# Loading each head pair's q, k and v one batch ahead in a fused sparse-attention and MLP kernel

## The chip, the cores and the metric

The kernel runs on one core of a Trainium2 chip. The metric is the device time of one execution in microseconds (us). A core has engines that work in order, each on its own stream of instructions: TensorE (PE, with its weight loads PEld), VectorE (DVE), ScalarE (ACT), GpSimd (POOL) and SyncE (SP). They wait for one another through semaphores. Transfers between DRAM and the on-chip memory are issued here by POOL (all loads) and SP (all stores).

## The reference

Attention over 8 batches, 8 heads, 576 positions of 64 channels. Heads 0 to 3 see only the last 32 positions (local); heads 4 to 7 see only earlier positions with the same remainder modulo 32 (strided). The heads' outputs, side by side, are the 4608 tokens of an MLP with a squared ReLU.

```python
B, H, S, D = q.shape                      # 8, 8, 576, 64
scores = (1.0 / np.sqrt(D)) * np.matmul(q, k.transpose(0, 1, 3, 2))
mask_local = (rel >= 0) & (rel < 32)
mask_strided = (rel >= 0) & (pos[None, :] % 32 == pos[:, None] % 32)
...
attn = softmax(np.where(mask, scores, -1e9))
x = np.matmul(attn, v).transpose(0, 2, 1, 3).reshape(B * S, H * D)
h = x @ w_in                              # 512 -> 2048
g = np.maximum(h, 0.0) ** 2
return g @ w_out                          # 2048 -> 512
```

## The kernel before, in words

**Attention** goes by pairs of heads: four pairs in each batch, two local (`attn_local_pair`, L162), then two strided (`attn_strided_pair`, L241). Each function first issues the pair's loads on POOL's queue. q and k come as float32 and are cast to bfloat16 on the way, one DMA for each head and tensor (L166 and L168, or L247 and L249, into `qb` and `kb`). v comes as four DMAs for a local pair (L181, L186, into `vt`) and as ten for a strided pair (L256, into five tiles `svwb`). So a local pair has eight loads and a strided pair fourteen. Then PE transposes q and k, nine small matmuls each, into one PSUM tile `ptr` (L175 or L264), and DVE copies them out as `qT2` and `kT2` (L177 or L266). In two groups of tiles follow: scores on PE (`psc`, L201 or L283), exponential on ACT (L126, L131), mask product with row sum on DVE (L135), the reciprocal as a diagonal matrix on DVE (L148, L157), a product on PE that transposes and scales at once (`pat`, L220 or L302), its copy on ACT (L227, L310), the product with v on PE (`po`, L233 or L322) and its copy by DVE into `xt` (L238 or L336), where all tokens lie with channels in partitions.

**The MLP** goes by nine chunks of 512 tokens, each in four quarters of the first product (`moe_mm1_quarter`, L340) and one second product (`moe_mm2`, L357). The first product accumulates, for each of 16 groups of hidden channels, four matmuls into `psh` (L349), one for each pair's rows of `xt` and each 128-row slab of `w_in_b`; ACT applies the ReLU (L353) and DVE squares (L354). The second accumulates 16 matmuls into `psy` (L363); ACT copies (L367) and SP stores.

**The weights** are loaded by POOL too: after each of the first pairs of batch 0, seven steps of `emit_weight_load` (L108), that is four slabs of `w_in_b` (L110) and three of `w_out_b` (L114) after pair 0, seven more of `w_out_b` after pair 1 and the last six after pair 2.

**Setup.** POOL writes two identity matrices and then three masks, `mask_loc_g0`, `mask_loc_g1` and `mask_str` (L61 to L99), twelve instructions, before the first load.

**Order.** The main loop (L392) takes batches and pairs in turn, and hands out MLP steps between pairs: none after the pairs of batch 0, two after each later pair, one after each batch; what is left comes at the end. The framework in which the kernel is written keeps, for each name of a tile, a number of buffers: four for `qb` and for `kb` (L41), 21 for `vt` and for `svwb` (L42), one for `ptr`, `po`, `psh` and `psy`, two for `psc` and `pat`. A new tile waits until the oldest buffer of its name has been read by all its users. The framework also fixes, when the program is built, the order of each engine's stream: it goes by the order in which the code emits the instructions, and may move one ahead of earlier ones where it reckons that those are not ready. On the chip each engine then keeps that order.

Of the kernel before, what the change touches and what calls it, by code (L numbers as in the profile page):

```python
# [11 lines left out]
BF16 = mybir.dt.bfloat16  # L12
AF = mybir.ActivationFunctionType
ALU = mybir.AluOpType
# [3 lines left out]
def kernel(  # L18
# [9 lines left out]
    nc = tc.nc  # L28
    B, H, S, D = q.shape
# [6 lines left out]
    QL = 96  # L36
    NLT = S // QL
# [4 lines left out]
    vw_pool = ctx.enter_context(tc.tile_pool(name="vw_pool", bufs=21))  # L42
# [16 lines left out]
    identr = ident_f  # L59

    mask_loc_g0 = singles.tile([96, 4, 128], BF16)  # L61
    nc.gpsimd.memset(mask_loc_g0, 1.0)
    nc.gpsimd.affine_select(
        out=mask_loc_g0, in_=mask_loc_g0, compare_op=ALU.is_ge, fill=0.0,
        base=-1, channel_multiplier=-1, pattern=[[0, 4], [1, 128]],
    )
    nc.gpsimd.affine_select(
        out=mask_loc_g0, in_=mask_loc_g0, compare_op=ALU.is_ge, fill=0.0,
        base=32, channel_multiplier=1, pattern=[[0, 4], [-1, 128]],
    )  # L70
    nc.gpsimd.memset(mask_loc_g0[:, 0, :], 1.0)
    nc.gpsimd.affine_select(
        out=mask_loc_g0[:, 0, :], in_=mask_loc_g0[:, 0, :], compare_op=ALU.is_ge,
        fill=0.0, base=0, channel_multiplier=1, pattern=[[-1, 128]],
    )
    nc.gpsimd.affine_select(
        out=mask_loc_g0[:, 0, :], in_=mask_loc_g0[:, 0, :], compare_op=ALU.is_ge,
        fill=0.0, base=31, channel_multiplier=-1, pattern=[[1, 128]],
    )
    mask_loc_g1 = singles.tile([96, 2, 128], BF16)  # L80
    nc.gpsimd.memset(mask_loc_g1, 1.0)
    nc.gpsimd.affine_select(
        out=mask_loc_g1, in_=mask_loc_g1, compare_op=ALU.is_ge, fill=0.0,
        base=-1, channel_multiplier=-1, pattern=[[0, 2], [1, 128]],
    )
    nc.gpsimd.affine_select(
        out=mask_loc_g1, in_=mask_loc_g1, compare_op=ALU.is_ge, fill=0.0,
        base=32, channel_multiplier=1, pattern=[[0, 2], [-1, 128]],
    )
    mask_str = singles.tile([126, 126], BF16)  # L90
    nc.gpsimd.memset(mask_str, 1.0)
    nc.gpsimd.affine_select(
        out=mask_str, in_=mask_str, compare_op=ALU.is_ge, fill=0.0,
        base=0, channel_multiplier=1, pattern=[[-18, 7], [-1, 18]],
    )
    nc.gpsimd.affine_select(
        out=mask_str, in_=mask_str, compare_op=ALU.is_ge, fill=0.0,
        base=17, channel_multiplier=-1, pattern=[[18, 7], [0, 18]],
    )  # L99

    xt = []
    for p in range(4):
# [56 lines left out]
                scalar1=rinv[0:w, 0, :], scalar2=None, op0=ALU.mult)  # L159
        return e_m, diag4  # L160

    def attn_local_pair(b, h0):  # L162
        qb = qkv_in.tile([64, 9, 2, D], BF16, name="qb")
        kb = qkv_in.tile([64, 9, 2, D], BF16, name="kb")
        for hh in range(2):
            nc.gpsimd.dma_start(out=qb[:, :, hh, :], in_=q[b, h0 + hh]  # L166
                                .rearrange("(j p) d -> p j d", p=64))
            nc.gpsimd.dma_start(out=kb[:, :, hh, :], in_=k[b, h0 + hh]  # L168
                                .rearrange("(j p) d -> p j d", p=64))
        qT2 = attn_sb.tile([128, 640], BF16, name="qT2")  # L170
        kT2 = attn_sb.tile([128, 640], BF16, name="kT2")
        for src_b, dst_t in ((qb, qT2), (kb, kT2)):
            ptr = ps_tr.tile([128, 576], BF16, name="ptr")
            for j in range(9):
                nc.tensor.transpose(ptr[:, 64 * j:64 * (j + 1)], src_b[:, j, :, :],  # L175
                                    ident[0:64, 0:64])
            nc.vector.tensor_copy(dst_t[:, 0:576], ptr)  # L177

        vt = vw_pool.tile([128, 6, 2, D], BF16, name="vt")
        for hh in range(2):  # L180
            nc.gpsimd.dma_start(out=vt[:, 0, hh, :], in_=v[b, h0 + hh, 0:128, :])  # L181
            vsrc = v[b, h0 + hh]
            win = dataclasses.replace(
                vsrc, offset=vsrc.offset + 64 * D,
                ap=[[D, 128], [QL * D, 5], [1, D]])
            nc.gpsimd.dma_start(out=vt[:, 1:6, hh, :], in_=win)  # L186
        vws = [vt[:, a, :, :] for a in range(NLT)]

        for g, gn in ((0, 4), (1, 2)):
            po = ps_o.tile([128, 512], FP32, name="po")  # L190
            pscs, sms, ats = [], [], []
            for hh in range(2):
                rbase = 64 * hh
                qTh = qT2[rbase:rbase + 64, :]
                kTh = kT2[rbase:rbase + 64, :]
                psc = ps_s.tile([128, 512], FP32, name="psc")
                ps_sc = psc[0:96, :].rearrange("p (t c) -> p t c", c=128)
                for t in range(gn):
                    a = 4 * g + t
                    lo = 0 if a == 0 else QL * a - 32  # L200
                    nc.tensor.matmul(  # L201
                        ps_sc[:, t, :],
                        qTh[:, QL * a:QL * a + 96],
                        kTh[:, lo:lo + 128],
                        start=True, stop=True,
                    )
                pscs.append(psc)
            mask = mask_loc_g0 if g == 0 else mask_loc_g1
            for hh in range(2):
                ps_sc = pscs[hh][0:96, :].rearrange("p (t c) -> p t c", c=128)  # L210
                sms.append(softmax_T(
                    ps_sc, [96] * gn, gn,
                    [mask[:, t, :] for t in range(gn)], [96, 4, 128]))
            pats = []
            for hh in range(2):
                e_m, diag4 = sms[hh]
                pat = ps_at.tile([128, 512], FP32, name="pat")
                ps_att = pat[:, 0:384].rearrange("p (t c) -> p t c", c=96)
                for t in range(gn):
                    nc.tensor.matmul(  # L220
                        ps_att[:, t, :], e_m[0:96, t, :], diag4[0:96, t, 0:96],
                        start=True, stop=True,
                    )
                pats.append(ps_att)
            for hh in range(2):
                at_sb = attn_sb.tile([128, 4, 96], BF16, name="at_sb")
                nc.scalar.copy(at_sb[:, 0:gn, :], pats[hh][:, 0:gn, :])  # L227
                ats.append(at_sb)
            for hh in range(2):
                ps_ot = po[64 * hh:64 * hh + 64, 0:384].rearrange(  # L230
                    "p (t c) -> p t c", c=96)
                for t in range(gn):
                    nc.tensor.matmul(  # L233
                        ps_ot[:, t, :], vws[4 * g + t][:, hh, :],
                        ats[hh][:, t, :], start=True, stop=True,
                    )
            dst = xt[h0 // 2][:, b * S + QL * 4 * g: b * S + QL * (4 * g + gn)]
            nc.vector.tensor_copy(  # L238
                dst, po[:, 0:96 * gn])

    def attn_strided_pair(b, h0):  # L241
        src_v = v[b, h0:h0 + 2].rearrange("h (a r) d -> r a h d", r=STRIDE)
        qb = qkv_in.tile([64, 9, 2, D], BF16, name="qb")
        kb = qkv_in.tile([64, 9, 2, D], BF16, name="kb")
        vrb = []
# [5 lines left out]
        for t in range(5):  # L251
            nt = SST[t]
            nr = nt // NB
            vwb = vw_pool.tile([128, 2, D], BF16, name="svwb")
            for hh in range(2):
                nc.gpsimd.dma_start(out=vwb[0:nt, hh, :],  # L256
                                    in_=src_v[7 * t:7 * t + nr, :, hh, :])
            vrb.append(vwb)
        qT2 = attn_sb.tile([128, 640], BF16, name="qT2")
        kT2 = attn_sb.tile([128, 640], BF16, name="kT2")  # L260
        for src_b, dst_t in ((qb, qT2), (kb, kT2)):
# [120 lines left out]
    def drain_moe(n):  # L382
        for _ in range(n):
            if not moe_steps:
                return
            c, step = moe_steps.pop(0)
            if step < 4:
                moe_mm1_quarter(c, step)
            else:
                moe_mm2(c)  # L390

    for b in range(B):  # L392
        for hp in range(H // 2):
            if hp < H // 4:
                attn_local_pair(b, 2 * hp)
            else:
                attn_strided_pair(b, 2 * hp)
            for _ in range(7):
                emit_weight_load(wstep)
                wstep += 1  # L400
            drain_moe(2 if b > 0 else 0)
        while next_chunk < NCHUNK and (512 * next_chunk + 511) // S <= b:
            moe_chunk(next_chunk)
            next_chunk += 1
        drain_moe(1)
# [34 lines left out]
```

The softmax here doesn't subtract the row's maximum and nothing guards it: scores larger than these inputs give would overflow.

## Time and profile before

| | |
|---|---|
| time, median of 4 runs | 511.46 us (509.35 to 511.82) |
| time of the profiled execution | 511.93 us |
| span of the profiled execution, first to last instruction | 510.1 us |
| mean granted TensorE clock | 0.949 |
| DMA, software queue (POOL's) | 152,896 packets, 19.27 MB |

In the rows below, L12 is line 12 of the kernel before. `A <- B` after an operation names the tile written and the tiles read; "x9" counts instructions that a row merges; in square brackets stands how long the engine was idle before the row and what ended that idle time. A row of the table of waits gives the engine and line that waited, what for, the total in us, the number of times and the longest.

### The profile page before, as it was taken

To read this page: it belongs to the slowest core of one execution; us is meant where nothing else is said; L and a number is where in the kernel's file an instruction comes from. 1 tells how busy PE (TensorE), PEld (TensorE's weight loads), DVE (VectorE), ACT (ScalarE), POOL (GpSimd) and SP (SyncE) were. 2 spreads that over 40 slices of the span, in tenths; PEclk is the share of its full clock that TensorE was granted. 3 is DMA by queue.
4 is the path that set the end of the run, shared out by engine and by line. 5 is a ranking of instruction groups with operands and counts; after the bars stand their busy time and mean duration, and the time that the engine had idled before them with its cause. 6 is when DMAs were issued, how large, how long until landed. Compare 5 with 4: busy or idle time off the path is not lost.

```text
span 510.1 us, 8132 instructions
## 1 busy us (share of the span) xinstructions
PE 412.9 (81%) x2784; PEld 198.3 (39%) x2784; DVE 281.4 (55%) x1232; ACT 196.8 (39%) x437; POOL 253.9 (50%) x392
## 2 busy tenths in 40 slices
PE   1344489897989798979897998799889986779775
PEld 1233334443444344434443444344434442224222
DVE  0445568746783678467845775577557763220210
ACT  1222235533543354245523553355235522332321
POOL 9499999985487699977344526443100000000000
PEclk9999999997999799979987999799979997999999
DMA  5999999987669879999455555545310011001001
GB/s 36 196 143 97 69 59 62 95 85 67 39 55 92 69 43 60 109 80 58 29 82 49 32 36 68 68 30 35 54 42 1 2 42 42 0 2 61 21 22 62
DMA packets 158121, 29.23 MB, mean 57 GB/s; under 512 B 150912, under 2 KB 152960, under 8 KB 158080
## 3 DMA queue, kind: packets, MB, share of 16 engines
q0 software_dynamic: 152896, 19.27, 53.9%
q1 hardware_dynamic: 5184, 9.44, 5.2%
q8 instruction: 22, 0.36, 0.3%
q14 instruction: 19, 0.16, 0.1%
HBM read 38.27 MB, written 9.44 MB: 94 GB/s over the span
## 4 chain that ended last, share of the span: by engine, by line
PE 65%; POOL 11%; ACT 8%; DVE 7%; issue 4%; DMA 3%; POOLq 0%; ACTq 0%
PE psh L349 30%; PE psy L363 22%; ACT r_sb L353 7%; DVE xt L336 7%; POOL svwb L256 3%; PE po L233 3%; PE po L322 2%; DMA w_in_b<-in_moe_w_in_dram 2%; PE psc L201 2%; PE pat L302 2%; PE pat L220 2%; PE ptr L175 1%; POOL w_out_b L114 1%; PE ptr L264 1%; POOL vt L186 1%
## 5 line engine op out<-in xcount | busy, mean ns | idle before, releaser
L349 PE MATMUL psh<-xt,w_in_b 128*128 128x512 bf16 x576 | 171.5, 410 | 22.4 <-ACT r_sb L353 16.8
L363 PE MATMUL psy<-w_out_b,g_sb 128*128 128x512 bf16 x576 | 154.6, 386 | 3.2 <-ACT y_sb L367 2.3
L353 ACT ACTIVATE r_sb<-psh 128x512 bf16<-128x512 f32 x144 | 86.0, 597 | 147.8 <-PE psh L349 146.6
L256 POOL DMA_DIRECT2D svwb<-in_v_dram x160 | 100.4, 788 | 23.8 <-PE pat L302 15.7
L354 DVE TENSOR_TENSOR g_sb<-r_sb 128x512 bf16<-128x512 bf16 x144 | 60.2, 418 | 82.3 <-ACT r_sb L353 82.1
L349 PEld LDWEIGHTS <-w_in_b 128*128 128x128 bf16 x576 | 53.4, 101 | 78.8 <-issue 41.5
L363 PEld LDWEIGHTS <-g_sb 128*128 128x128 bf16 x576 | 55.4, 99 | 66.4 <-issue 7.2
L336 DVE CAST xt<-po 128x504 bf16<-128x504 f32 (+1 forms) x32 | 45.0, 1408 | 48.2 <-PE po L322 47.8
L126 ACT ACTIVATE e_sb<-psc 96x512 bf16<-96x512 f32 (+2 forms) x96 | 44.8, 517 | 36.9 <-PE psc L201 22.7
L367 ACT COPY y_sb<-psy 128x512 f32<-128x512 f32 x36 | 21.1, 586 | 93.1 <-PE psy L363 75.2
L148 DVE TENSOR_TENSOR diag<-ident,rinv 96x384 bf16<-96x384 bf16 (+2 forms) x96 | 50.3, 524 | 0.3
L135 DVE CUSTOM_DVE_ANT_0 e_m<-e_sb,mask_loc_g 96x128 bf16<-96x128 bf16 x192 | 46.4, 276 | 4.6 <-ACT e_sb L126 4.2
L135 DVE CUSTOM_DVE_ANT_0 e_m<-e_sb,mask_str 126x126 bf16<-126x126 bf16 (+1 forms) x160 | 36.0, 269 | 21.4 <-ACT e_sb L131 11.9
L322 PE MATMUL po<-sat_sb,svwb 126*64 126x126 bf16 (+1 forms) x160 | 16.3, 232 | 33.5 <-DVE xt L336 12.4
L168 POOL DMA_DIRECT2D kb<-in_k_dram x32 | 26.5, 832 | 25.2 <-PE ptr L175 18.4
L249 POOL DMA_DIRECT2D kb<-in_k_dram x32 | 28.0, 880 | 22.2 <-PE ptr L264 22.0
L247 POOL DMA_DIRECT2D qb<-in_q_dram x32 | 28.1, 883 | 16.7 <-PE ptr L264 16.1
L166 POOL DMA_DIRECT2D qb<-in_q_dram x32 | 27.3, 867 | 15.9 <-PE ptr L175 14.2
L186 POOL DMA_DIRECT2D vt<-in_v_dram x32 | 33.0, 1033 | 0.4 <-issue 0.2
L227 ACT CAST at_sb<-pat 128x384 bf16<-128x384 f32 (+1 forms) x64 | 25.0, 396 | 11.8 <-PE pat L220 11.2
L135 DVE DVE_READ_ACCUMULATOR2_ANT ssum<- 96x1 f32 (+2 forms) x352 | 27.9, 79 | 0.0
L322 PEld LDWEIGHTS <-svwb 126*64 126x64 bf16 (+1 forms) x160 | 9.9, 114 | 44.8 <-issue 17.4
(52 smaller groups left out, 375.8 us busy)
## 6 DMA issues: line engine op xcount, KB each, us to landing
out_dram<-y_sb SPq DMA_DIRECT2D x36, 256.0 KB, 2.1
qb<-in_q_dram POOLq DMA_DIRECT2D x64, 72.0 KB, 2.9
kb<-in_k_dram POOLq DMA_DIRECT2D x64, 72.0 KB, 3.0
vt<-in_v_dram POOLq DMA_DIRECT2D x32, 80.0 KB, 3.0
w_in_b<-in_moe_w_in_dram POOLq DMA_DIRECT2D x4, 512.0 KB, 8.6
w_out_b<-in_moe_w_out_dram POOLq DMA_DIRECT2D x16, 128.0 KB, 4.1
svwb<-in_v_dram POOLq DMA_DIRECT2D x128, 15.8 KB, 2.4
vt<-in_v_dram POOLq DMA_DIRECT2D x32, 16.0 KB, 2.6
```

The source lines that it names most:

```text
L126: nc.scalar.activation(e_sb[:, 0:gn, :], ps_sc[:, 0:gn, :], AF.Exp, scale=scale)
L135: nc.vector.tensor_tensor_reduce(out=e_m[0:w, t, 0:mask3[t].shape[-1]], in0=e_sb[0:w, t, 0:mask3[t].shape[-1]], in1=mask3[t], scale=1.0, s ...
L148: nc.vector.tensor_tensor(diag4[0:w, 0:gn, 0:w], id_b, rinv[0:w, 0:gn, :].to_broadcast([w, gn, w]), op=ALU.mult)
L186: nc.gpsimd.dma_start(out=vt[:, 1:6, hh, :], in_=win)
L247: nc.gpsimd.dma_start(out=qb[:, :, hh, :], in_=q[b, h0 + hh] .rearrange("(j p) d -> p j d", p=64))
L256: nc.gpsimd.dma_start(out=vwb[0:nt, hh, :], in_=src_v[7 * t:7 * t + nr, :, hh, :])
L322: nc.tensor.matmul(ps_ot[:, t, 0:nt], vrb[tt][0:nt, hh, :], ats[hh][0:nt, t, 0:nt], start=True, stop=True)
L336: nc.vector.tensor_copy(dst, src)
L349: nc.tensor.matmul(psh[:, 0:cw], w_in_b[:, kk, 128 * ff:128 * (ff + 1)], xt[kk][:, cols], start=(kk == 0), stop=(kk == 3))
L353: nc.scalar.activation(r_sb[:, 0:cw], psh[:, 0:cw], AF.Relu)
L354: nc.vector.tensor_tensor(g_sb[:, ff, 0:cw], r_sb[:, 0:cw], r_sb[:, 0:cw], op=ALU.mult)
L363: nc.tensor.matmul(psy, g_sb[:, ff, 128 * j:128 * (j + 1)], w_out_b[:, ff, :], start=(ff == 0), stop=(ff == 15))
```

## The change

The loads of a pair move out of the two attention functions into `load_local_pair` and `load_strided_pair`, which return the tiles. The loads of all four pairs of batch 0 are emitted ahead of the main loop, and the masks, now in a function `emit_masks`, between those of pair 0 and those of pair 1. In the loop, after a pair's attention and its weight loads, the loads of the same pair of the next batch are emitted. The instructions themselves, their number and the numbers of buffers stay.

```diff
-    nc.gpsimd.memset(mask_loc_g0, 1.0)
...
+    def emit_masks():
+        nc.gpsimd.memset(mask_loc_g0, 1.0)
...
-    def attn_local_pair(b, h0):
+    def load_local_pair(b, h0):
         qb = qkv_in.tile([64, 9, 2, D], BF16, name="qb")
...
+        vt = vw_pool.tile([128, 6, 2, D], BF16, name="vt")
...
+        return qb, kb, vt
+
+    def attn_local_pair(b, h0, loaded):
+        qb, kb, vt = loaded
+        vws = [vt[:, a, :, :] for a in range(NLT)]
...
-    def attn_strided_pair(b, h0):
+    def load_strided_pair(b, h0):
...
+        return qb, kb, vrb
+
+    def attn_strided_pair(b, h0, loaded):
+        qb, kb, vrb = loaded
...
+    pending = {}
+    for hp in range(H // 2):
+        pending[(0, hp)] = (load_local_pair if hp < H // 4 else
+                           load_strided_pair)(0, 2 * hp)
+        if hp == 0:
+            emit_masks()
     for b in range(B):
         for hp in range(H // 2):
+            loaded = pending.pop((b, hp))
             if hp < H // 4:
-                attn_local_pair(b, 2 * hp)
+                attn_local_pair(b, 2 * hp, loaded)
             else:
-                attn_strided_pair(b, 2 * hp)
+                attn_strided_pair(b, 2 * hp, loaded)
             for _ in range(7):
                 emit_weight_load(wstep)
                 wstep += 1
+            if b + 1 < B:
+                pending[(b + 1, hp)] = (load_local_pair if hp < H // 4 else
+                                        load_strided_pair)(b + 1, 2 * hp)
             drain_moe(2 if b > 0 else 0)
```

More of the change, by code (lines that the diff above doesn't have):

```diff
@@ L61 @@
     mask_loc_g0 = singles.tile([96, 4, 128], BF16)
[L62 to L79, printed above, removed]
-    mask_loc_g1 = singles.tile([96, 2, 128], BF16)
[L81 to L89, printed above, removed]
-    mask_str = singles.tile([126, 126], BF16)
[L91 to L99, printed above, removed]
+    mask_loc_g1 = singles.tile([96, 2, 128], BF16)
@@ new lines @@
+    mask_str = singles.tile([126, 126], BF16)
+    def emit_masks():
+        nc.gpsimd.memset(mask_loc_g0, 1.0)
+        nc.gpsimd.affine_select(
+            out=mask_loc_g0, in_=mask_loc_g0, compare_op=ALU.is_ge, fill=0.0,
+            base=-1, channel_multiplier=-1, pattern=[[0, 4], [1, 128]],
+        )
+        nc.gpsimd.affine_select(
+            out=mask_loc_g0, in_=mask_loc_g0, compare_op=ALU.is_ge, fill=0.0,
+            base=32, channel_multiplier=1, pattern=[[0, 4], [-1, 128]],
+        )
+        nc.gpsimd.memset(mask_loc_g0[:, 0, :], 1.0)
+        nc.gpsimd.affine_select(
+            out=mask_loc_g0[:, 0, :], in_=mask_loc_g0[:, 0, :],
+            compare_op=ALU.is_ge,
+            fill=0.0, base=0, channel_multiplier=1, pattern=[[-1, 128]],
+        )
+        nc.gpsimd.affine_select(
+            out=mask_loc_g0[:, 0, :], in_=mask_loc_g0[:, 0, :],
+            compare_op=ALU.is_ge,
+            fill=0.0, base=31, channel_multiplier=-1, pattern=[[1, 128]],
+        )
+        nc.gpsimd.memset(mask_loc_g1, 1.0)
+        nc.gpsimd.affine_select(
+            out=mask_loc_g1, in_=mask_loc_g1, compare_op=ALU.is_ge, fill=0.0,
+            base=-1, channel_multiplier=-1, pattern=[[0, 2], [1, 128]],
+        )
+        nc.gpsimd.affine_select(
+            out=mask_loc_g1, in_=mask_loc_g1, compare_op=ALU.is_ge, fill=0.0,
+            base=32, channel_multiplier=1, pattern=[[0, 2], [-1, 128]],
+        )
+        nc.gpsimd.memset(mask_str, 1.0)
+        nc.gpsimd.affine_select(
+            out=mask_str, in_=mask_str, compare_op=ALU.is_ge, fill=0.0,
+            base=0, channel_multiplier=1, pattern=[[-18, 7], [-1, 18]],
+        )
+        nc.gpsimd.affine_select(
+            out=mask_str, in_=mask_str, compare_op=ALU.is_ge, fill=0.0,
+            base=17, channel_multiplier=-1, pattern=[[18, 7], [0, 18]],
+        )
@@ L169, in attn_local_pair @@
                                 .rearrange("(j p) d -> p j d", p=64))
+        vt = vw_pool.tile([128, 6, 2, D], BF16, name="vt")
+        for hh in range(2):
+            nc.gpsimd.dma_start(out=vt[:, 0, hh, :], in_=v[b, h0 + hh, 0:128, :])
+            vsrc = v[b, h0 + hh]
+            win = dataclasses.replace(
+                vsrc, offset=vsrc.offset + 64 * D,
+                ap=[[D, 128], [QL * D, 5], [1, D]])
+            nc.gpsimd.dma_start(out=vt[:, 1:6, hh, :], in_=win)
+        return qb, kb, vt
+    def attn_local_pair(b, h0, loaded):
+        qb, kb, vt = loaded
+        vws = [vt[:, a, :, :] for a in range(NLT)]
         qT2 = attn_sb.tile([128, 640], BF16, name="qT2")
@@ L177, in attn_local_pair @@
             nc.vector.tensor_copy(dst_t[:, 0:576], ptr)
[L179 to L187, printed above, removed]
         for g, gn in ((0, 4), (1, 2)):
```

## The prediction, made before the result

> **What bounds the kernel now.** I read the page's first two parts, then a table of stretches of the span, then the timeline of the opening by engine. First the page: shares by engine, then forty slices.
>
> ```profile
> PE 412.9 (81%) x2784; PEld 198.3 (39%) x2784; DVE 281.4 (55%) x1232; ACT 196.8 (39%) x437; POOL 253.9 (50%) x392
> ...
> PE   1344489897989798979897998799889986779775
> POOL 9499999985487699977344526443100000000000
> ```
>
> PE is the busiest engine, but its digits show two regimes: 1 to 4 in the first five slices (some 64 us), 8 to 9 afterwards. POOL, which issues every load, is the reverse: full at the start, resting later. So the stretches are looked at separately. Columns: window, its length, then busy time of PE, PEld, DVE, ACT, POOL, then granted clock and DMA.
>
> ```profile
> core 0: us, PE busy (x) PEld busy (x) DVE busy (x) ACT busy (x) POOL busy (x), PEclk, DMA share, GB/s
> 0.00:10.20 10.20, 0.00 (x0) 0.00 (x0) 0.00 (x0) 1.28 (x1) 9.56 (x27) 1.00 0.45 28
> 10.20:21.00 10.80, 6.09 (x55) 4.00 (x55) 6.37 (x36) 3.31 (x8) 7.34 (x12) 1.00 1.05 163
> 21.00:28.10 7.10, 0.00 (x0) 0.00 (x1) 0.00 (x0) 0.00 (x0) 3.73 (x6) 1.00 1.54 183
> 28.10:38.87 10.77, 6.03 (x56) 4.04 (x56) 6.37 (x36) 3.34 (x8) 10.53 (x18) 1.00 1.36 135
> 118.77:170.30 51.53, 46.47 (x332) 22.42 (x332) 33.96 (x153) 22.79 (x52) 33.82 (x51) 0.93 0.76 64
> 429.40:510.10 80.70, 61.84 (x252) 24.62 (x251) 13.62 (x32) 23.11 (x39) 0.00 (x0) 0.97 0.07 26
> ```
>
> A batch of the middle takes 51.5 us with PE busy for 46.5 of them, and the end is MLP work alone: both are limited by PE and its evacuations. The first 10.2 us and the 7.1 us from 21.00 have no PE work at all. I call the four head pairs of batch 0 pairs 0 to 3 (0 and 1 local, 2 and 3 strided). PE's timeline (start, busy, line, operation, then the idle time before it and who ended it):
>
> ```profile
> 10.26 0.64 PE L175 MATMUL ptr<-ident,qb 64*128 64x64 bf16 x9 [10.26 <-DMA qb<-in_q_dram]
> ...
> 20.41 0.59 PE L349 MATMUL psh<-xt,w_in_b 128*128 128x512 bf16 x1 [0.46 <-DVE xt L238]
> 28.10 0.66 PE L175 MATMUL ptr<-ident,qb 64*128 64x64 bf16 x9 [7.10 <-DMA qb<-in_q_dram]
> ...
> 38.35 0.58 PE L349 MATMUL psh<-xt,w_in_b 128*128 128x512 bf16 x1 [0.45 <-DVE xt L238]
> 38.87 0.66 PE L264 MATMUL ptr<-ident,qb 64*128 64x64 bf16 x9
> ...
> 52.87 0.66 PE L264 MATMUL ptr<-ident,qb 64*128 64x64 bf16 x9
> ...
> 55.85 0.69 PE L283 MATMUL psc<-kT,qT 64*126 64x126 bf16 x8 [0.85 <-DVE kT L266]
> ...
> 63.15 0.23 PE L175 MATMUL ptr<-ident,qb 64*128 64x64 bf16 x1
> ...
> 66.37 0.59 PE L349 MATMUL psh<-xt,w_in_b 128*128 128x512 bf16 x1
> ```
>
> The four pairs run one behind another. Pair 0 takes 10.26 to 21.00, pair 1 28.10 to 38.87 (10.77), pair 2 38.87 to 52.87 (14.00), pair 3 52.87 to 66.37 (13.50). Behind each pair stands one matmul of the MLP's first group, which takes one slab of w_in_b each; with the fourth, at 66.37, MLP work really begins. Both long gaps end with the landing of a qb. Who holds the qb up is on POOL's timeline:
>
> ```profile
> 1.68 0.52 POOL L62 MEMSET mask_loc_g<- 96x512 bf16 x1
> ...
> 5.65 0.86 POOL L166 DMA_DIRECT2D qb<-in_q_dram  x1
> ...
> 7.23 0.74 POOL L166 DMA_DIRECT2D qb<-in_q_dram  x1
> ...
> 11.48 2.23 POOL L110 DMA_DIRECT2D w_in_b<-in_moe_w_in_dram  x4
> ...
> 15.18 0.89 POOL L166 DMA_DIRECT2D qb<-in_q_dram  x1
> 17.53 0.75 POOL L168 DMA_DIRECT2D kb<-in_k_dram  x1 [1.46 <-DMA w_in_b<-in_moe_w_in_dram]
> 20.01 0.73 POOL L166 DMA_DIRECT2D qb<-in_q_dram  x1 [1.74 <-DMA w_in_b<-in_moe_w_in_dram]
> 22.45 0.73 POOL L168 DMA_DIRECT2D kb<-in_k_dram  x1 [1.71 <-DMA w_in_b<-in_moe_w_in_dram]
> 24.91 0.58 POOL L181 DMA_DIRECT2D vt<-in_v_dram  x1 [1.73 <-DMA w_in_b<-in_moe_w_in_dram]
> ...
> 27.93 3.75 POOL L114 DMA_DIRECT2D w_out_b<-in_moe_w_out_dram  x7
> 31.61 0.82 POOL L247 DMA_DIRECT2D qb<-in_q_dram  x1
> ...
> 34.54 3.82 POOL L256 DMA_DIRECT2D svwb<-in_v_dram  x6
> ...
> 40.92 3.28 POOL L114 DMA_DIRECT2D w_out_b<-in_moe_w_out_dram  x6
> ...
> 53.16 0.89 POOL L166 DMA_DIRECT2D qb<-in_q_dram  x1
> ```
>
> POOL makes masks from 1.68 to 5.65, issues pair 0's eight loads from 5.65 to 11.48, then seven weight loads, and then stands four times, before one of pair 1's loads each, until one of the four w_in_b transfers has landed. Pair 1's second qb thus leaves at 20.01, its last load just before 27.93. That is the whole of the gap at 21.00. Later the loads are not late; there POOL waits for the kernel:
>
> ```profile
> POOL kb L168 <- PE ptr L175: 18.4, 8, 5.8
> ```
>
> Eight waits, 18.4 us, for transposes to free a buffer: loads already run four pairs ahead as far as the four buffers allow. The change keeps the four buffers, so I cost the middle and the end at nothing, and look for all of the effect in the first 66 us.
>
> **The change part by part.**
>
> *Masks behind pair 0's loads.* Their 3.97 us (1.68 to 5.65) go from before the first load to behind it, so pair 0's first transposes should stand at 10.26 - 3.97 = 6.29. What is late next is the mask. POOL finishes the eight loads at 1.68 + 5.83 = 7.51 (5.83 from 5.65 to 11.48) and all masks at 11.48. In the trace the first masked product is this:
>
> ```profile
> 13.98 0.29 DVE L135 CUSTOM_DVE_ANT_0 e_m<-e_sb,mask_loc_g 96x128 bf16<-96x128 bf16 x1 [1.41 <-ACT e_sb L126]
> ```
>
> It would be due at 13.98 - 3.97 = 10.01, so it waits up to 1.47 us. On DVE all later work of the pair queues behind it, and PE's next product after that. Net for pair 0: 3.97 - 1.47 = 2.50 us; it ends at 18.50. (If only the three local masks count, the wait is about a quarter of a microsecond less; I keep the full set.)
>
> *Pair 1's loads ahead of the weights.* They start at 11.48, right behind the masks; the second qb leaves 1.58 us later (7.23 - 5.65), at 13.06. Pair 0's second qb left at 7.23 and its transposes ran at 10.26, 3.03 later; so pair 1 is ready at 16.1, ahead of 18.50. The 7.10 us gap goes. Sum so far: 2.50 + 7.10 = 9.60.
>
> *Pairs 2 and 3's loads ahead of the weights.* Pair 1's loads end at 11.48 + 5.83 = 17.31. A strided pair's fourteen loads took 9.31 (31.61 to 40.92): pair 2's run to 26.62, pair 3's to 35.93. Served one behind another, the pairs stand at 18.50, 29.27, 43.27 and 56.77, so both sets lie ready well ahead. This permits what could not happen before: a pair's transposes and their copies, 2.98 us from 52.87 to 55.85, put into the idle spots of the pair ahead, as the one transpose at 63.15 was put into pair 3. For each of pairs 2 and 3 this is worth 0 to 2.98. I take one of the two, 3.0, since pair 3's q and k are there some ten microseconds before its turn and pair 2's only five or so. Sum: 12.6.
>
> *Weights behind three pairs' loads.* w_in_b now leaves at 35.93 instead of 11.48, 24.45 us later. Landings were at 17.5, 20.0, 22.5 and 24.9 (the ends of POOL's four waits); they become 42.0, 44.5, 46.9 and 49.4. The last is needed by the fourth matmul, at 56.77 or a little earlier: covered by about four to seven microseconds. The first slabs are covered only if their matmul does not stand in PE's queue too early; this is the rival below. POOL's four waits now fall on pair 4's loads (the first of batch 1): 35.93 + 3.70 for seven weight loads (11.48 to 15.18) + 12.75 (15.18 to 27.93) = 52.4 for its last load, and its q and k some five microseconds earlier, which fits a PE that gets there between 53 and 57. Loads of pairs 5 to 7 are issued in the same total time as before, while PE asks for them about 13 us earlier; in a batch of 51.5 us each pair adds 12.9 of demand against 6 to 9 of issue, so they stay ahead. w_out_b's last slab moves by a few microseconds and is used only in the second MLP product. No instruction is added or removed.
>
> *POOL beside DVE.* Three pairs' issues and the masks now run beside busy vector work. With DVE idle two issues took 1.58 (5.65 to 7.23), 0.79 each; beside 6.37 us of DVE work in 10.77 four took 2.93 (31.61 to 34.54), 0.73 each. So I cost this at nothing. The Trainium skill's page "SBUF — State Buffer", section "SBUF: two separate sides", speaks against the change here: a DMA issued from GpSimd needs descriptors written through a port that it shares with the vector engine, so some vector work holds the issue back. If all DVE work of pairs 0 and 1 did so, 2 x 6.37 = 12.7 us would come on top of POOL's issues, the last w_in_b would land at 62.1, and of the saving 4.3 would be left; these rows show no such slowing.
>
> The sum is for the profiled execution: span 510.1, own time 511.93, 0.1% above the median of the runs, 511.46. 510.1 - 12.6 = 497.5 of span, 499.3 of time; from the median, 498.9. I say 499.
>
> **The rivals.**
>
> *More overlap.* Both hoists work and part of the scores as well. The floor is the last slab of w_in_b: the matmul of 66.37 cannot run ahead of 49.4, a saving of at most 17.0: 494.5. For it: PE is busy only 6.0 of 10.8 us in a pair, so there is room. Against: the rows of batch 0 show only one such hoist.
>
> *PE's queue blocks on w_in_b.* PE works in order, and the single MLP matmul now behind pair 0 (20.41) was placed by a compile-time order; its weights had landed, for it waited for xt alone. If it keeps a place ahead of pair 2, at 29.27, it stands until 42.0, 12.7 us, with three pairs' attention behind it: 12.7 - 9.6 = 3.1 slower, 514.6. If it keeps its place behind pair 0, at 18.50, it loses 23.5: 13.9 slower, 525. From pair 2's end (43.27) on it costs at most the spacing of the slabs, about 4 us, and the change still gains 6. Against it: the order is made with the loads' new places known, and a matmul is put where its inputs are expected. It decides if w_in_b's transfer is expected much faster than it is.
>
> *Given back, or no effect.* The opening gets shorter, but batch 1 finds pair 4's loads late, or the middle settles into another order: seven middle batches that are 1.5 us longer eat 10.5. Also, loads were prefetched already. Time 510 to 513. Against: the gap of 7.10 us is real, and nothing of POOL's work is needed at a fixed time later.
>
> **How the numbers follow.** More overlap 0.20; the forecast, a saving of 8 to 14, 0.50; its weaker form with waits on slabs, a saving of 3 to 8, 0.12; given back or no effect 0.08; PE blocked and slower 0.10. About 0.5%, 2.6 us, is what a measurement can tell here (the four runs shown span 509.35 to 511.82). So faster 0.82, same 0.08, slower 0.10. The range takes more overlap to its floor, 494, and the weaker form to a saving of 3.5, 508; some 0.2 is left out, nearly all above.
>
> **What would show it.** Right: first transposes near 6.3; the first masked product waiting for POOL's masks near 11; no gap between pair 0 and pair 1; the four POOL waits on w_in_b now from about 40 to 50; the fourth lone MLP matmul near 54; middle batches still about 51.5 and the end 80.7. Wrong: a lone L349 matmul before 40 whose wait is ended by w_in_b, a gap ahead of pair 4's first transposes, or middle batches over 53 us.

## The result and the profile after

The changed kernel takes 494.73 us (median of 11 runs, 492.23 to 496.28) against 511.16 us before (15 runs, 509.13 to 512.20). The ratio is 0.9675, with a 95% interval of 0.9656 to 0.9694: 16.4 us less. The profiled execution has a span of 494.6 us and a time of 496.28 us, which is the slow end of the eleven. Lines of the changed kernel have other numbers: L170 and L172 are the local pair's q and k loads, L176 and L181 its `vt`, L254 and L256 the strided pair's, L263 `svwb`, L114 `w_in_b`, L118 `w_out_b`, L192 and L275 the transposes, L139 the mask product, L208 and L294 the scores, L333 the strided product with v, L347 its copy, L360 and L374 the two MLP products, L364 the ReLU. In the experiments' kernels some of these are a few lines further down.

The page's first parts of the changed kernel:

```profile
PE 413.9 (84%) x2784; PEld 199.7 (40%) x2784; DVE 281.2 (57%) x1232; ACT 197.2 (40%) x437; POOL 254.1 (51%) x392
...
PE   2664899879999999799879988998979996779775
...
POOL 9994999999874789789626263523000000000000
```

Work is the same; PE's low digits now last four slices of 12.4 us, where they lasted five of 12.8. Next the table of stretches, cut at the point where the MLP's first full group of four matmuls starts, first before the change, then after it (columns as in the prediction):

```profile
0.00:67.64 67.64, 25.13 (x227) 17.69 (x227) 30.09 (x138) 14.31 (x34) 59.90 (x105) 1.00 1.09 107
67.64:221.62 153.98, 139.16 (x997) 66.93 (x996) 102.39 (x458) 68.27 (x156) 126.81 (x191) 0.95 0.89 71
221.62:429.42 207.80, 186.74 (x1310) 89.09 (x1310) 135.37 (x608) 91.15 (x208) 67.22 (x99) 0.93 0.42 43
```

```profile
0.00:50.38 50.38, 24.78 (x208) 17.68 (x209) 28.32 (x137) 14.23 (x34) 43.34 (x78) 1.00 0.93 90
50.38:206.06 155.68, 140.54 (x1014) 68.29 (x1014) 103.96 (x458) 68.69 (x156) 136.35 (x207) 0.94 1.02 85
206.06:413.88 207.82, 186.75 (x1311) 89.08 (x1311) 135.38 (x608) 91.17 (x208) 74.40 (x109) 0.93 0.45 45
413.88:494.60 80.72, 61.84 (x252) 24.62 (x251) 13.57 (x32) 23.10 (x39) 0.00 (x0) 0.97 0.07 26
```

The opening is 17.26 us shorter (67.64 to 50.38) with nearly the same PE work in it. PEld's count falls by eighteen (227 to 209): the transposes of pair 4, the first pair of batch 1, now stand behind the cut. The next three batches are 1.70 us longer, 1.38 of it PE's own busy time with those eighteen in it; from there on the two kernels run alike to 0.1 us. PE's timeline of the opening after the change:

```profile
6.25 0.64 PE L192 MATMUL ptr<-ident,qb 64*128 64x64 bf16 x9 [6.25 <-DMA qb<-in_q_dram]
...
16.16 0.21 PE L192 MATMUL ptr<-ident,qb 64*128 64x64 bf16 x1 [1.24 <-DMA qb<-in_q_dram]
...
23.42 0.66 PE L275 MATMUL ptr<-ident,qb 64*128 64x64 bf16 x9
...
33.72 0.28 PE L275 MATMUL ptr<-ident,qb 64*128 64x64 bf16 x2
...
44.08 0.62 PE L360 MATMUL psh<-xt,w_in_b 128*128 128x512 bf16 x1
...
48.24 1.46 PE L360 MATMUL psh<-xt,w_in_b 128*128 128x512 bf16 x3
50.38 1.86 PE L360 MATMUL psh<-xt,w_in_b 128*128 128x512 bf16 x4 [0.69 <-ACT r_sb L364]
```

The pairs' first transposes stand 9.9, 7.3 and 10.3 us apart, where the kernel before had 17.8, 10.8 and 14.0: pairs 1, 2 and 3 start inside the pair ahead of them. POOL's timeline:

```profile
1.71 0.86 POOL L170 DMA_DIRECT2D qb<-in_q_dram  x1
...
11.56 0.77 POOL L170 DMA_DIRECT2D qb<-in_q_dram  x1
...
14.48 0.63 POOL L176 DMA_DIRECT2D vt<-in_v_dram  x1
...
35.12 2.49 POOL L114 DMA_DIRECT2D w_in_b<-in_moe_w_in_dram  x4
...
41.26 0.75 POOL L172 DMA_DIRECT2D kb<-in_k_dram  x1 [1.29 <-DMA w_in_b<-in_moe_w_in_dram]
43.41 0.72 POOL L170 DMA_DIRECT2D qb<-in_q_dram  x1 [1.41 <-DMA w_in_b<-in_moe_w_in_dram]
45.88 0.73 POOL L172 DMA_DIRECT2D kb<-in_k_dram  x1 [1.74 <-DMA w_in_b<-in_moe_w_in_dram]
48.45 0.58 POOL L176 DMA_DIRECT2D vt<-in_v_dram  x1 [1.84 <-DMA w_in_b<-in_moe_w_in_dram]
```

POOL's four waits for w_in_b are still there, but they now hold up pair 4's loads, while PE still has pair 3 to do.

### The profile page after: what moved, and what is told of

It is laid out like the page before. It is cut to its first block, busy times and chain, and to the rows that moved or that the text cites. A ratio compares the mean times of both kernels' runs of the same rounds, so it can differ in the third digit from the quotient of the medians.

```text
span 494.6 us, 8124 instructions
## 1 busy us (share of the span) xinstructions
PE 413.9 (84%) x2784; PEld 199.7 (40%) x2784; DVE 281.2 (57%) x1232; ACT 197.2 (40%) x437; POOL 254.1 (51%) x392
## 4 chain that ended last, share of the span: by engine, by line
PE 59%; POOL 16%; ACT 8%; DVE 7%; DMA 6%; issue 4%; POOLq 0%; ACTq 0%
PE psh L360 26%; PE psy L374 20%; ACT r_sb L364 7%; POOL svwb L263 6%; DVE xt L347 6%; PE po L240 3%; DMA w_in_b<-in_moe_w_in_dram 2%; PE po L333 2%; POOL kb L256 2%; POOL vt L181 2%; PE psc L208 2%; DMA kb<-in_k_dram 2%; POOL qb L254 2%; PE pat L227 1%; PE pat L313 1%
## 5 line engine op out<-in xcount | busy, mean ns | idle before, releaser
L360 PE MATMUL psh<-xt,w_in_b 128*128 128x512 bf16 x576 | 168.9, 406 | 22.8 <-ACT r_sb L364 18.7
L374 PE MATMUL psy<-w_out_b,g_sb 128*128 128x512 bf16 x576 | 156.5, 390 | 5.1 <-ACT y_sb L378 2.7
L364 ACT ACTIVATE r_sb<-psh 128x512 bf16<-128x512 f32 x144 | 86.0, 597 | 137.7 <-PE psh L360 135.7
L263 POOL DMA_DIRECT2D svwb<-in_v_dram x160 | 99.1, 706 | 23.2 <-PE pat L313 15.7
L360 PEld LDWEIGHTS <-w_in_b 128*128 128x128 bf16 x576 | 53.5, 101 | 82.2 <-issue 45.1
L374 PEld LDWEIGHTS <-g_sb 128*128 128x128 bf16 x576 | 56.0, 99 | 71.0 <-issue 10.7
L347 DVE CAST xt<-po 128x504 bf16<-128x504 f32 (+1 forms) x32 | 45.0, 1408 | 40.7 <-PE po L333 40.4
L139 DVE CUSTOM_DVE_ANT_0 e_m<-e_sb,mask_str 126x126 bf16<-126x126 bf16 (+1 forms) x160 | 36.0, 268 | 29.0 <-ACT e_sb L130 16.4
L139 DVE CUSTOM_DVE_ANT_0 e_m<-e_sb,mask_loc_g 96x128 bf16<-96x128 bf16 x192 | 46.9, 279 | 5.9 <-POOL mask_loc_g L81 2.8
L333 PE MATMUL po<-sat_sb,svwb 126*64 126x126 bf16 (+1 forms) x160 | 16.3, 235 | 26.5 <-DVE xt L347 15.5
L172 POOL DMA_DIRECT2D kb<-in_k_dram x32 | 26.2, 820 | 23.2 <-PE ptr L192 19.3
L256 POOL DMA_DIRECT2D kb<-in_k_dram x32 | 25.3, 796 | 19.8 <-PE ptr L275 18.0
L254 POOL DMA_DIRECT2D qb<-in_q_dram x32 | 25.7, 810 | 12.5 <-PE ptr L275 12.5
L170 POOL DMA_DIRECT2D qb<-in_q_dram x32 | 27.3, 863 | 8.8 <-PE ptr L192 6.6
L234 ACT CAST at_sb<-pat 128x384 bf16<-128x384 f32 (+1 forms) x64 | 25.0, 396 | 16.2 <-PE pat L227 15.5
L181 POOL DMA_DIRECT2D vt<-in_v_dram x32 | 30.7, 958 | 0.6 <-DMA w_out_b<-in_moe_w_out_dram 0.5
L139 DVE DVE_READ_ACCUMULATOR2_ANT ssum<- 96x1 f32 (+2 forms) x352 | 28.1, 80 | 0.0
L333 PEld LDWEIGHTS <-svwb 126*64 126x64 bf16 (+1 forms) x160 | 9.9, 115 | 38.6 <-issue 22.4
```

The costliest lines, as they stand in the source:

```text
L139: nc.vector.tensor_tensor_reduce(out=e_m[0:w, t, 0:mask3[t].shape[-1]], in0=e_sb[0:w, t, 0:mask3[t].shape[-1]], in1=mask3[t], scale=1.0, s ...
L254: nc.gpsimd.dma_start(out=qb[:, :, hh, :], in_=q[b, h0 + hh] .rearrange("(j p) d -> p j d", p=64))
L263: nc.gpsimd.dma_start(out=vwb[0:nt, hh, :], in_=src_v[7 * t:7 * t + nr, :, hh, :])
L333: nc.tensor.matmul(ps_ot[:, t, 0:nt], vrb[tt][0:nt, hh, :], ats[hh][0:nt, t, 0:nt], start=True, stop=True)
L347: nc.vector.tensor_copy(dst, src)
L360: nc.tensor.matmul(psh[:, 0:cw], w_in_b[:, kk, 128 * ff:128 * (ff + 1)], xt[kk][:, cols], start=(kk == 0), stop=(kk == 3))
```

## The experiments

Two theories stood against each other. **Chain:** the opening is the attention of four pairs, one behind another on PE, DVE and ACT; what counts is when each pair's loads are there, and the weights must stand where no pair waits behind them. **Queue, in its strong form:** POOL's total of issues up to batch 1 is the bound, in whatever order. All ratios are to the kernel before, run on the same chip in the same session; the last three columns come from each run's profile.

| run | ratio (95% interval) | pair 1's first transposes | MLP's first full group | span |
|---|---|---|---|---|
| before | 1 | 28.10 | 67.64 | 510.1 |
| changed | 0.9675 (0.9656 to 0.9694) | 16.16 | 50.38 | 494.6 |
| masks only | 0.9967 (0.9942 to 0.9993) | 27.55 | 66.72 | 507.8 |
| masks first | 0.9729 (0.9691 to 0.9766) | 16.00 | 51.81 | 496.0 |
| weights first | 0.9803 (0.9761 to 0.9844) | 27.51 | 60.29 | 500.9 |
| pair 1 only | 0.9995 (0.9972 to 1.0018) | 16.20 | 67.81 | 509.5 |
| loop as before | 0.9731 (0.9694 to 0.9767) | 16.04 | 50.27 | 495.2 |
| POOL 4 us | 0.9698 (0.9668 to 0.9727) | 16.07 | 51.50 | 494.8 |
| w_in_b spread | 0.9717 (0.9688 to 0.9747) | 15.97 | 50.47 | 495.2 |
| mask before v | 0.9696 (0.9666 to 0.9726) | 16.23 | 50.45 | 495.3 |
| POOL order | 0.9695 (0.9672 to 0.9718) | 14.74 | 50.63 | 493.1 |
| late, same order | 0.9693 (0.9664 to 0.9722) | 16.14 | 50.39 | 492.0 |

**Masks only.** In these diffs `load` and `attn` stand for the changed kernel's load and attention functions of one pair.

```diff
+            load(b, hp)
+            if b == 0 and hp == 0:
+                emit_masks()
             attn(b, hp)
             # the seven weight loads, as before
```

> The kernel before with one edit: the masks are made behind pair 0's loads instead of ahead of them; weights and all other loads stay where they were. Chain theory (as in the prediction: each saving in the opening counts by itself): pair 0 ends 2.5 us earlier, so 508.7 us. Queue theory (what counts is when POOL gets each later load out): pair 1's loads leave POOL at the same moment as before, so pair 0 only waits longer for pair 1; no change, 511.2 us, and the gap before pair 1 grows from 7.1 to 9.6 us.

PE's timeline of this run:

```profile
6.45 0.64 PE L192 MATMUL ptr<-ident,qb 64*128 64x64 bf16 x9 [6.45 <-DMA qb<-in_q_dram]
...
27.55 0.66 PE L192 MATMUL ptr<-ident,qb 64*128 64x64 bf16 x9 [9.08 <-DMA qb<-in_q_dram]
```

Pair 0 starts 3.8 us earlier, and the gap ahead of pair 1 grows from 7.10 to 9.08 us. Of the 2.5 us by which pair 0 ends earlier (its lone MLP matmul ends at 18.47, before at 21.00), 0.9 reach the MLP's start: alone, the masks' move buys mostly idle time. The time fell by 0.3% (0.1 to 0.6%), some 1.7 us; the interval is clear of zero and takes in the chain theory's 2.5, but the timeline is nearer to the queue theory.

**Masks first.**

```diff
+    emit_masks()
     for hp in range(H // 2):
         load(0, hp)
-        if hp == 0:
-            emit_masks()
```

> The changed kernel with the masks back ahead of pair 0's loads; the rest as changed. Chain theory: pair 0 ends 2.5 us later and everything behind it too, 497.2 us. Queue theory: POOL gets every load of pairs 1 to 3 and every weight out at the same moment as in the changed kernel, so only pair 0 is late and pair 1, which stood ready at 16.2 us at the earliest, hides most of it: 494.7 to 495.7 us.

The time, 497.65 us, is within half a microsecond of the chain theory's 497.2 and outside the other's range, but the ratios' intervals overlap, and the MLP starts only 1.4 us later than in the changed kernel. At the MLP's start the masks' move is thus worth more with pair 1's loads in place than alone (1.4 to 0.9), but not the full 2.5 us: pair 1's transposes stand at 16.00 here and at 16.16 there. What the rest of the time is was not found.

**Weights first.**

```diff
     load(0, 0)
     emit_masks()
+    for _ in range(7):
+        emit_weight_load(wstep); wstep += 1
     for hp in range(1, H // 2):
         load(0, hp)
     ...
             attn(b, hp)
+            if (b, hp) != (0, 0):
                 # the seven weight loads, as before
```

> The changed kernel with the first seven weight loads (all of w_in_b) put back ahead of pair 1's loads; masks and all later loads as changed. Chain theory: pair 1 starts at 28 us again, the 7.1 us gap is back, pairs 2 and 3 still overlap for 3 to 6 us: about 505 us (503 to 508). Queue theory in its strong form (POOL's total until the loads of batch 1 is the bound, in whatever order): 495 to 497 us, although the gap at 21 us is back.

```profile
27.51 0.66 PE L192 MATMUL ptr<-ident,qb 64*128 64x64 bf16 x9 [9.04 <-DMA qb<-in_q_dram]
...
33.55 0.66 PE L275 MATMUL ptr<-ident,qb 64*128 64x64 bf16 x9
...
43.85 0.29 PE L275 MATMUL ptr<-ident,qb 64*128 64x64 bf16 x2
```

The gap is back, and pairs 2 and 3 start 6.0 and 10.3 us behind the pair ahead of them, not 10.8 and 14.0. The time, 501.95 us, lies just under the chain theory's 503 to 508 and clear of the 495 to 497 of the strong queue theory, which falls.

**Pair 1 only.**

```diff
     load(0, 0)
     emit_masks()
+    load(0, 1)
     for b in range(B):
         for hp in range(H // 2):
+            if (b, hp) not in ((0, 0), (0, 1)):
+                load(b, hp)
             attn(b, hp)
             # the seven weight loads, as before
```

> Only pair 1's loads go ahead of the weights (and the masks behind pair 0's loads); pairs 2 and 3 and all later batches are loaded where the kernel before did it. Chain theory: the gap of 7.1 us goes, but the four waits for w_in_b now fall on pair 2's loads; pair 2 can start at about 31.5, pair 3 at about 45.5, the MLP at about 59 instead of 66.4: about 504 us. Queue theory in its strong form: 495 to 497 us.

Both theories missed this one. POOL's timeline, and then PE's:

```profile
19.44 2.23 POOL L118 DMA_DIRECT2D w_out_b<-in_moe_w_out_dram  x4
23.94 0.54 POOL L118 DMA_DIRECT2D w_out_b<-in_moe_w_out_dram  x1 [2.27 <-DMA w_in_b<-in_moe_w_in_dram]
26.39 0.53 POOL L118 DMA_DIRECT2D w_out_b<-in_moe_w_out_dram  x1 [1.92 <-DMA w_in_b<-in_moe_w_in_dram]
29.39 0.53 POOL L118 DMA_DIRECT2D w_out_b<-in_moe_w_out_dram  x1 [2.47 <-DMA w_in_b<-in_moe_w_in_dram]
31.32 1.82 POOL L118 DMA_DIRECT2D w_out_b<-in_moe_w_out_dram  x3 [1.39 <-DMA w_in_b<-in_moe_w_in_dram]
33.25 0.76 POOL L254 DMA_DIRECT2D qb<-in_q_dram  x1
```

```profile
39.07 0.66 PE L275 MATMUL ptr<-ident,qb 64*128 64x64 bf16 x9 [9.72 <-DMA qb<-in_q_dram]
```

Pair 1 runs early, and then PE stands 9.72 us ahead of pair 2 instead of 7.10 ahead of pair 1. I had reckoned that pair 2's first loads would follow the seven weight loads; with pair 1's loads gone from there, all fourteen weight loads come first, and POOL's waits fall on them. The gap was moved, not removed, and the gain is nothing. PE also stood for w_in_b itself here, when the lone MLP matmul behind pair 0 came to its weights (PEld's timeline):

```profile
23.70 0.10 PEld L360 LDWEIGHTS <-w_in_b 128*128 128x128 bf16 x1 [2.21 <-DMA w_in_b<-in_moe_w_in_dram]
```

Pair 1's first product with the diagonal matrix, queued behind it, starts at 24.10, where the changed kernel has it at 23.01. The gap that follows hides this loss.

**Loop as before, and late, same order.** The first emits the loads of batches 1 to 7 ahead of their own pair; the second does so for batches 2 to 7 only.

```diff
 # loop as before
+            if b > 0:
+                load(b, hp)
             attn(b, hp)
             ...
-            if b + 1 < B:
-                load(b + 1, hp)
```

```diff
 # late, same order
+            if b > 1:
+                load(b, hp)
             attn(b, hp)
             ...
-            if b + 1 < B:
+            if b == 0:
                 load(b + 1, hp)
```

> The changed kernel with the loads of batches 1 to 7 emitted right ahead of their own pair, as in the kernel before; only batch 0's loads stay up front. If the loop's part of the change does nothing, because four buffers already let loads run four pairs ahead: 494.7 us, as the changed kernel. If emitting them one batch ahead is worth something by itself: 497 us or more.

> The changed kernel with the loads of batches 2 to 7 emitted right ahead of their own pair, as before the change; batches 0 and 1 as changed. If the loads of the later batches are held by the four buffers and not by where they stand in the code, this is the changed kernel again: 494.7 us. If the place in the code counts: some other time, by 1 us or more.

In the second, every engine's stream of instructions is the changed kernel's, one for one, as far as the traces show it (47 of PE's 2784 matmul records are missing from the second; its weight loads are all there). So from batch 2 on the loop's part of the change does nothing: POOL has only loads left there, in the same order wherever the code emits them, and the buffers hold them back (its largest wait in total, 19.3 us, is that of `kb` at L172 for PE's transposes at L192). In the first, all weights go out ahead of pair 4's loads, and pair 4's first transposes come at 62.34 instead of 55.87:

```profile
62.34 0.43 PE L192 MATMUL ptr<-ident,qb 64*128 64x64 bf16 x9
```

Its ratio, 0.9731, is 0.4% above that of the second, with intervals that overlap; whether these 6.5 us cost a microsecond or two, or nothing, stays open.

**POOL 4 us, and w_in_b spread.** One makes w_in_b later, the other earlier.

```diff
 # POOL 4 us, behind pair 3's loads
+    scratch = singles.tile([128, 2048], BF16)
+    for _ in range(2):
+        nc.gpsimd.memset(scratch, 1.0)
...
 # w_in_b spread, in pair 3's loads of v, behind each tile's
+            if t < len(weights):
+                emit_weight_load(weights[t])
```

> The changed kernel with two fills of an unused tile, together some 4 us of POOL work, put behind pair 3's loads and about the first slab of w_in_b; nothing reads them. If the landing of w_in_b is what the MLP's start at 50.4 us hangs on (or ends level with pair 3's attention), the start moves to 53.5 to 54.4 and the time to 498 to 498.7. If it is hidden behind pair 3's attention with room to spare: 494.7 to 495.5.

> The changed kernel with the four slabs of w_in_b issued among pair 3's v loads, one after every two, instead of in one block behind them. If pair 3's chain of attention ends the opening by itself: the MLP starts within 0.7 us of 50.4 and the time is 494 to 494.7. If w_in_b's landing ended it: 2 to 4 us earlier, 491 to 493. If the 1.7 us that were given back in batch 1 come from POOL's four waits for w_in_b (6.3 us together), they come back: about 493.

PE's timeline of the first, then of the second:

```profile
47.96 0.27 PE L333 MATMUL po<-sat_sb,svwb 72*64 72x72 bf16 x2 [2.31 <-DVE xt L347]
48.56 1.06 PE L360 MATMUL psh<-xt,w_in_b 128*128 128x512 bf16 x2 [0.33 <-issue]
50.21 0.61 PE L360 MATMUL psh<-xt,w_in_b 128*128 128x512 bf16 x1 [0.59 <-DMA w_in_b<-in_moe_w_in_dram]
51.50 1.86 PE L360 MATMUL psh<-xt,w_in_b 128*128 128x512 bf16 x4 [0.69 <-ACT r_sb L364]
```

```profile
48.37 0.27 PE L335 MATMUL po<-sat_sb,svwb 72*64 72x72 bf16 x2 [2.52 <-DVE xt L349]
49.21 0.58 PE L362 MATMUL psh<-xt,w_in_b 128*128 128x512 bf16 x1 [0.56 <-DVE xt L349]
50.47 1.87 PE L362 MATMUL psh<-xt,w_in_b 128*128 128x512 bf16 x4 [0.69 <-ACT r_sb L366]
```

Later weights: POOL's waits for the second to fourth slab end 2.0 to 2.1 us later than in the changed kernel (45.52, 47.98, 50.45), so only half of the fills' 4 us arrives; the fourth lone matmul waits for its slab, and the MLP starts 1.1 us later. Earlier weights: it waits for pair 3's copy, and nothing moves. So in the changed kernel the two end level, within about a microsecond, and pair 3's chain is the last. In time neither run can be told from the changed kernel, and the extra 4 us on POOL are mostly hidden: my 498 and more was wrong. So was the return of 1.7 us in the spread version, although all but 0.74 us of POOL's waits for w_in_b moved off batch 1's loads.

**Mask before v, and POOL order.** One makes the first mask among pair 0's v loads; the other also puts pair 1's q and k ahead of the second local mask, and the strided mask behind pair 2's loads.

`between` is called ahead of the pair's v loads.

```diff
 # mask before v
+    pending[(0, 0)] = load_local_pair(0, 0, between=emit_mask_g0)
+    emit_mask_rest()
...
 # POOL order
+    pending[(0, 0)] = load_local_pair(0, 0, between=emit_mask_g0)
+    pending[(0, 1)] = load_local_pair(0, 2, between=emit_mask_g1)
+    for hp in range(2, H // 2):
+        pending[(0, hp)] = load_strided_pair(0, 2 * hp)
+        if hp == 2:
+            emit_mask_str()
```

> The changed kernel with the first local mask made among pair 0's v loads, ahead of three of them, instead of behind all eight loads. Chain theory: the first masked product no longer waits the extra 1.4 us for POOL, v still lands before its use, and the gain carries through: 493.3 to 494. If pair 1's q and k (ready at 16.2 us) decide instead, nothing is gained: 494.7.

> The changed kernel with POOL's opening put in order of need: pair 0's q and k, the first local mask among pair 0's v loads, then pair 1's q and k, the second local mask among pair 1's v loads, and the strided mask behind pair 2's loads. If the opening now hangs on when pair 1's q and k leave POOL (its transposes stood at 16.2 us in the changed kernel and in every run with all four pairs ahead of the weights), they come about 1 to 1.5 us earlier and the MLP starts at about 49: 493 to 494 us. If pair 0's own attention or w_in_b's landing hold the rest: no change, 494.7.

DVE's timeline of the first:

```profile
10.25 0.48 DVE L141 CUSTOM_DVE_ANT_0 e_m<-e_sb,mask_loc_g 96x128 bf16<-96x128 bf16 x1 [1.73 <-POOL mask_loc_g L81]
...
10.66 0.57 DVE L141 CUSTOM_DVE_ANT_0 e_m<-e_sb,mask_loc_g 96x128 bf16<-96x128 bf16 x1
```

The first masked product comes 1.1 us earlier (10.25 for 11.36). But beside POOL's remaining mask instructions, products that otherwise take 0.28 us take up to 0.57, and PE's first product behind them comes only 0.44 us earlier (12.95 for 13.39), and pair 1's transposes stand at 16.23 as before. Nothing is gained.

PE's timeline of the second:

```profile
14.74 0.64 PE L198 MATMUL ptr<-ident,qb 64*128 64x64 bf16 x9 [1.53 <-DMA qb<-in_q_dram]
...
18.22 0.32 PE L233 MATMUL pat<-diag,e_m 96*128 96x96 bf16 x2 [0.91 <-DVE diag L156]
...
50.63 1.87 PE L366 MATMUL psh<-xt,w_in_b 128*128 128x512 bf16 x4 [0.69 <-ACT r_sb L370]
```

Pair 1's transposes come 1.4 us earlier, and the MLP no earlier. Pair 0's second group waits at 18.22 now, where the second mask was made late: its first masked product comes at 15.78, after POOL's last instruction for that mask (15.19 to 15.61), and came at 13.68 in the changed kernel. I argue that this took the gain, and did not try it. No version beats the changed kernel by what can be measured.

## Why the prediction was right, and what it mis-sized

It said 499.0 us, 494 to 508; measured were 494.73. The direction and the place, the opening alone, were right. By its steps:

**First transposes and masks.** 6.29 was forecast, 6.25 measured. The first masked product was put at 11.48 at the latest:

```profile
11.36 0.38 DVE L139 CUSTOM_DVE_ANT_0 e_m<-e_sb,mask_loc_g 96x128 bf16<-96x128 bf16 x1 [2.79 <-POOL mask_loc_g L81]
```

It waited for the first local mask alone, which the prediction's remark in brackets allowed for (there are two local masks, not three). But 2.50 us as a term of its own was wrong: masks only gave 0.9 us at the MLP's start, and undoing it in the changed kernel cost 1.4.

**The gap of 7.10 us.** Gone, as forecast; pair 1 was to be ready at 16.1, and stood at 16.16. Weights first brings it back. Counted at the MLP's start, from weights first to the changed kernel is 60.29 - 50.38 = 9.9 us. That is more than 7.10, because the gap in weights first is 9.04 us long, with the masks' saving in it, and because pair 1 now also starts inside pair 0. Masks and gap share their effect in this way; together they were put at 9.60, and the two steps measure 0.9 + 9.9.

**Overlap of pairs 2 and 3: the step that was mis-sized.** I took 3.0 us, one of two hoists. From masks only to weights first, where only the loads of pairs 2 and 3 (and later ones) come earlier, the MLP's start moves from 66.72 to 60.29: 6.4 us. Both hoists work. The three steps 0.9 + 6.4 + 9.9 make the 17.26 us of the opening, against 12.6 forecast. This was the rival "more overlap", with its floor of 494.5. That the time came out at this floor is in part luck: the floor was the landing of the last slab, and what came last was pair 3's chain, within a microsecond of it. Of the 4.6 us by which the opening beat the forecast, 3.4 belong to this term.

**Weights behind three pairs' loads.** w_in_b left at 35.12 (forecast 35.93) and its slabs were there by 41.3, 43.4, 45.9 and 48.5 (forecast 42.0 to 49.4). The cover of four to seven microseconds shrank to under one, since the fourth lone matmul came at 49 and not near 54.

**The rival on a blocked PE** did not come in the changed kernel: the lone matmuls stand at 44.08 and from 48.24, behind their slabs. In pair 1 only it did, for 2.21 us at 23.70, beside a gap that moved to the next pair.

**Given back.** 17.26 us in the opening became 15.5 of span in this profile (16.4 in the medians). Late, same order is the same stream of instructions, and its profile has the same opening (50.39). Its next three batches:

```profile
50.39:205.99 155.60, 138.20 (x998) 68.01 (x1015) 105.19 (x459) 68.63 (x156) 136.06 (x207) 0.95 1.01 85
```

They take 155.60 us, against 155.68 in the changed kernel's profile and 153.98 before. So the 1.7 us are given back in both, and the granted clock, here 0.95 as before the change, does not explain it. What the rows show is that pair 4's transposes have moved. Before, they stood at the end of the opening, in places where PE would have been idle (in the changed kernel it waits 0.69 us there, ahead of the full group); now they stand among the MLP's matmuls. Before the change, then after it:

```profile
65.74 0.60 PE L175 MATMUL ptr<-ident,qb 64*128 64x64 bf16 x8
...
66.89 0.65 PE L175 MATMUL ptr<-ident,kb 64*128 64x64 bf16 x9
```

```profile
55.87 0.43 PE L192 MATMUL ptr<-ident,qb 64*128 64x64 bf16 x9
...
57.15 0.43 PE L192 MATMUL ptr<-ident,kb 64*128 64x64 bf16 x9
```

That is 0.86 us of PE's time, about half of what is missing, and no run tests it; the rest stays open.

The clock shows up later. The twin's span is 492.0 us, 2.6 shorter than the changed kernel's, and all but 0.1 of that lies behind 206 us; the mean clocks of the two profiles are 0.950 and 0.944. Over the eleven runs of the changed kernel, those at 0.950 have spans of 490.5 to 491.7 us and those at 0.944 of 494.5 and 494.6. That denser work at the start lowers the clock is possible, and was not tested.

**POOL beside DVE.** Pair 1's four q and k loads, now issued while pair 0's vector work runs, took 2.92 us (11.56 to 14.48), against 2.93 and 0.73 each in the quoted rows of before; the loads of pairs 2 and 3 took 8.90 and 8.93 (17.29 to 26.19 to 35.12), against 9.31. The slowing that the Trainium skill's page "SBUF — State Buffer", section "SBUF: two separate sides", warns of was not seen. So costing it at nothing was right here; whether this kernel's vector work is of the kind that the page means, no run shows.

## What to carry to other kernels

A long transfer in a load queue costs whoever is behind it in the queue (here from the eighth load behind it on), not whoever uses it: put it behind everything that will be waited for first, and check that all of these are ahead of it, since moving only the first waiter's loads moves the gap to the second. When loads come early enough for the next unit's first step to run inside the present one, count that overlap for every unit, beside the gap itself. A saving ahead of a wait is worth little until the wait is gone (0.9 of 2.5 us here), so terms of an opening do not add up one by one.

## What the runs showed of the hardware

A POOL load that stands for w_in_b is in the traces of these runs the eighth load behind the slab it waits for: k behind four slabs, three w_out_b and one q in the changed kernel; the fifth w_out_b behind four slabs and four w_out_b in pair 1 only. Why the eighth was not tried. POOL's waits for the slabs end some 2.2 to 2.6 us apart (41.26, 43.41, 45.88, 48.45).

One and the same stream of instructions (the changed kernel and late, same order, 17 runs) took 492.23 to 496.97 us, in order of its granted clock: 0.950 at the fast end, 0.941 at the slow end. This spread of 1% is larger than most of the effects sought in the second half of the experiments.

The Trainium skill's page "DMA: Bandwidth & Descriptors", section "Issuing engines are not separate DMA queues", calls the time to start a DMA usually small beside the DMA itself. Here the starts add up: one takes POOL 0.6 to 0.9 us, where the page of the changed kernel's profile has 2.4 to 3.0 us from issue to landing for the loads of q, k and v. The eight loads of pair 0 took POOL from 1.71 to 7.54, and all four pairs' issues, with the masks, lasted until 35.12; that is what sets where w_in_b can stand.
